# Attention with a feed-forward layer on one core: the order of the row-tiled group, of the division, and which pairs run it

## The chip, the cores and the metric

The kernel runs on one core of one Trainium2 chip. The time is the device time of one execution in microseconds (us). A core has five engines that run beside each other: TensorE (PE in the profile; its weight loads are listed as PEld), VectorE (DVE), ScalarE (ACT), GpSimd (POOL) and SyncE (SP). Each works through its own queue in order and waits on semaphores for the others. DMA transfers are issued by SP and by POOL.

## The reference

Attention with a relative position bias, 8 batches of 8 heads, 576 tokens, head size 64, and behind it two dense layers with a leaky ReLU between them on the 4608 tokens (512 to 2048 to 512).

```python
scores = scale * np.matmul(q, k.transpose(0, 1, 3, 2))
...
scores = scores + bias.transpose(2, 0, 1)[None, :, :, :]
scores = scores - np.max(scores, axis=-1, keepdims=True)
attn = np.exp(scores)
attn = attn / (np.sum(attn, axis=-1, keepdims=True) + 1e-09)
attn_out = np.matmul(attn, v)
x = attn_out.transpose(0, 2, 1, 3).reshape(B * S, H * D)
h = x @ w_in
g = np.maximum(0.01 * h, h)
out = g @ w_out
```

## The kernel before

**Pairs.** The work is cut into 32 items, each a batch and a pair of heads; item n is batch n // 4, heads 2p and 2p + 1 with p = n % 4. "Pair n" is item n below, counted from 0, so the 9th pair is n = 8 and the 13th is n = 12. While the scores of pair n are computed, the values of pair n - 1 are.

**Attention of a pair.** `score(n, u)` has PE compute a block of transposed scores (keys in the partitions) and ScalarE its exponential into `at`. Blocks u = 0 to 3 are 128 keys of both heads against 512 queries (L312): two products of 64 rows each, one per head, one on each half of the rows of the array. They use the two buffers of `ps_s` in turn. Block 4 (L305) is the last 64 queries; it is written to the banks o0 and o1 (`ps_q`). Block 5 (L315, L316) is the last 64 keys of both heads, with all 128 rows. `band(n, u)` multiplies the bias factor into the middle of a block on DVE (L348). The values of a head have a column of ones, so the row sum comes out beside the result. `av_tails` (L361) are the products of the last 64 keys into o0 and o1, row-tiled (each on 64 of the 128 rows), and `av` (L372) the others with all rows, a head after the other. `divide` (L380, L381) takes reciprocals and multiplies, which fills `opair`. `x_transposes` turns `opair` into `xT`, the tokens' input of the dense layers: by DMA from SP (L421), or for some pairs on PE (L428) with a copy on DVE (L429). `transpose_q` and `transpose_k` (L290, L294) make the next pair's `qt` and `kt`, from pair 9 on out of `turned`, which a DMA from SP fills (`turn_by_dma`, L265) after DVE has packed the rows (`pair_rows`, L257).

**The dense layers.** They are cut into pieces of four products of 512 columns and put between the steps of the pairs. An "in" piece (`ffn_in`, L454) is 128 of the 2048 hidden units for a tile of 512 tokens and ends in a leaky ReLU on ScalarE (`leaky`, L467). An "out" piece (`ffn_out`, L481) is a quarter of the sum for 128 tokens; the fourth is followed by a copy to `y` on DVE (L499) and a store from SP (L500). They use the two banks of tag "m", and now and then o0 (`spare`). `plan(n)` decides how many pieces a pair gets (seven or eight from pair 7 on) and what kind may run; what is over when the pairs are done runs in `moe_rest`.

**Two bodies.** `body_in_halves` is run for a pair where `both(n)` holds: in the program before for the 17 pairs n = 9, 13, 14, 17, 18, 19 and 21 to 31. There everything from score block 0 to score block 4 is row-tiled. The value products are split into two halves of the rows (`av_phase`): in phase 0 rows 0 to 63 work for the first head, into o0, while rows 64 to 127 work for the second, into o1; in phase 1 the other way round. Beside them an "in" and an "out" piece are done in halves in the same way (`open_two`, L598 and L601): a phase has four steps c, each of two products of 512 columns on the two halves of the rows. The two halves may not write the same bank at once, so phase 1 has to wait for the end of phase 0: `fence` puts an instruction on SP that waits for the last product of phase 0 (L389), and `behind` makes the first product of phase 1 wait for that. There are two such fences in a pair, for the values and for the pieces. All other pairs go through the body in the loop at the end, where `av` runs with all 128 rows between row-tiled scores and tails; there the first head is divided before the second one's products. Pairs 8 and 12 run there with the plan `lead`: eight out pieces, of which four stand between the value products (`slot`), with the copy to `y` on ScalarE.

**Order.** The order on every engine is the order in which the program issues (`manual_schedule`). So what is written first waits first, and what stands behind it in the same engine's queue waits with it.

Of the kernel before, what the change touches and what calls it, by code (L numbers as in the profile page):

```python
# [37 lines left out]
def kernel(  # L38
# [221 lines left out]
    def by_dma(n):  # L260
        return n > 2 * n_pairs
# [103 lines left out]
    def av(n, e):  # L365
        b, p = items[n]
        at = at_[n % 2]
        ps = outs[n][e][:, 0 : (NJ + 1) * (D + 1)].rearrange("p (i d) -> p i d", d=D + 1)
        for ic in range(NJ + 1):
            for c in range(NJ):  # L370
                o = (e * NJ + c) * S + ic * P
                nc.tensor.matmul(ps[:, ic, :], lhsT=at[:, o : o + P], rhs=vn[b % NBUF][:, c, 2 * p + e, :],  # L372
                                 start=False, stop=(ic == NJ and c == NJ - 1))
        divide(n, e)

    def divide(n, e):
        opair = ops_[n]
        ps = outs[n][e][:, 0 : (NJ + 1) * (D + 1)].rearrange("p (i d) -> p i d", d=D + 1)
        rcp = rc_pool.tile([P, NJ + 1, 1], FP32, name="rcp")
        nc.vector.reciprocal(rcp, ps[:, :, D : D + 1])  # L380
        nc.vector.tensor_tensor(out=opair[:, :, e * D : (e + 1) * D], in0=ps[:, :, 0:D],  # L381
                                in1=rcp.to_broadcast([P, NJ + 1, D]), op=ALU.mult)

    halves = (slice(0, P // 2), slice(P // 2, P))
    ended = mybir.DependencyInfo(mybir.DependencyClass.Sync, mybir.DependencyReason.DATA)
# [27 lines left out]
    def x_by_dma(n):  # L413
        return n_pairs + 2 <= n < N - 1 and n != 2 * n_pairs - 1

    def x_transposes(n):
        b, p = items[n]
        opair = ops_[n]
        w = (NJ + 1) * P
        if x_by_dma(n):  # L420
            nc.sync.dma_start_transpose(  # L421
                out=xT[p][:, b * S : b * S + w].rearrange("p (i t) -> p i t", t=P),
                in_=opair.rearrange("p i d -> p (i d)"),
            )
            return
        ps = ps_m_pool.tile([P, 8 * P], BF16, name="ps_tx", tag="m")
        for ic in range(NJ + 1):
            nc.tensor.transpose(ps[:, ic * P : (ic + 1) * P], in_=opair[:, ic, :], identity=ident)  # L428
        nc.vector.tensor_copy(out=xT[p][:, b * S : (b + 1) * S], in_=ps[:, 0:S])  # L429
# [28 lines left out]
    def leaky(T, f, pm, by_vector=False, between=None):  # L458
        g = gts[T][:, f, :]
        if by_vector:  # L460
            low = low_pool.tile([P, TT], BF16, name="low")
            nc.vector.tensor_scalar(low, pm, 0.01, None, op0=ALU.mult)
            if between is not None:
                between()
            nc.vector.tensor_tensor(out=g, in0=low, in1=pm, op=ALU.max)
        else:
            nc.scalar.activation(g, pm, AF.Prelu, bias=0.0, scale=1.0, alpha=0.01)  # L467
# [50 lines left out]
    def step(kind):  # L518
        T, s = made[kind], at_piece[kind]
        at_piece[kind] = (s + 1) % n_fc  # L520
        if at_piece[kind] == 0:
            made[kind] += 1
        return T, s

    def piece_out():
        T, s = step("out")
        ffn_out(T, s)
# [52 lines left out]
        elif room["left"] > room["keep"]:  # L580
            moe(1)

    def open_two():

        (Ti, f), (To, s) = step("in"), step("out")
        assert s % 4 == 0 and f < n_fc
        if f == 0:
            gts[Ti] = gt_pool.tile([P, n_fc, TT], BF16, name="gt")
        pi, po = bank("pm1"), bank("pm2")
        outs_pm[To] = po  # L590
        ti, ts = Ti * TT, (s // 4) * P

        def phase(k, lo, hi, last=None):
            for c in range(lo, hi):
                for r in range(2):
                    h = halves[r]
                    if r == k:
                        m = nc.tensor.matmul(pi, lhsT=w_in_sb[h, c, f * P : (f + 1) * P], rhs=xT[c][h, ti : ti + TT],  # L598
                                         start=(k == 0 and c == 0), stop=(k == 1 and c == n_cc - 1))
                    else:  # L600
                        m = nc.tensor.matmul(po, lhsT=gts[To][h, c, ts : ts + P], rhs=w_out_sb[h, c, :],  # L601
                                         start=(k == 0 and c == 0), stop=False)
                    if last is not None:
                        behind(m, last)
                        last = None
            return m

        return phase, lambda: leaky(Ti, f, pi)

    def both(n):  # L610
        return (by_dma(n) and n < N and can("in") and can("out") and at_piece["out"] % 4 == 0
                and not room["only"] and not room["split"] and not room["lead"] and room["left"] >= 6)

    def body_in_halves(n):

        loads(n)
        turns = rows_ahead(n) if by_dma(n + 1) else []
        for u in range(2):
            score(n, u)
        av_tails(n - 1)  # L620
        last = fence(av_phase(n - 1, 0))
        phase, low = open_two()
        phase(0, 0, 2)
        av_phase(n - 1, 1, last)
        if n + 1 < N:
            transpose_q(n + 1)
        band(n, 0)
        divide(n - 1, 0)
        divide(n - 1, 1)
        last = fence(phase(0, 2, n_cc))  # L630
        score(n, 2)
        score(n, 3)
        phase(1, 0, n_cc, last)
        band(n, 1)
        if n + 1 < N:
            transpose_k(n + 1)
        score(n, 4)
        low()
        for m in turns:
            turn_by_dma(m)  # L640
        x_transposes(n - 1)
        while stores:
            o, y = stores.pop(0)
            nc.sync.dma_start(out=o, in_=y)
        if not x_by_dma(n - 1):
            finished(n - 1)
        band(n, 2)
        piece_out()
        band(n, 4)
        score(n, 5)  # L650
        band(n, 5)
        piece_out()
        piece_out()
        room["left"] -= 5
        moe(room["left"], 0)

# [99 lines left out]
    def score(n, u):  # L756
        exp(n, u, qk_mm(n, u))
# [69 lines left out]
    for n in range(n_pairs + 1, N + 1):  # L827
        live = n < N
        more = n + 1 < N
        if x_by_dma(n - 2):  # L830
            finished(n - 2)
        plan(n)
        if live and both(n):
            body_in_halves(n)
            continue
        if live:
            begin(n)
            ps_a, ps_b = qk_mm(n, 0), qk_mm(n, 1)
# [48 lines left out]
        block = moe_block()  # L887
        next(block)
        exp(n, 3, ps_b)
        next(block)  # L890
        exp(n, 4, ps_c)
        if can("out"):
            next(block)
        band(n, 4)
        ps_a = qk_mm(n, 5)
        exp(n, 5, ps_a)
        band(n, 5)
        for _ in block:
            pass
# [31 lines left out]
```

## Time and profile before

| | |
|---|---|
| Time, median of 3 runs | 375.07 us (373.76, 375.07, 375.43) |
| The profiled execution's own time | 374.44 us |
| Its span | 372.5 us |
| PE busy | 358.1 us (96%) |
| ACT busy | 241.4 us (65%) |
| DVE busy | 198.8 us (53%) |
| Mean granted TensorE clock | 1.000 |

The span runs from the first to the last instruction, and the times of the views count from its start. In a row of the timeline stand the start, the length, the engine, the line, the operation with what it writes and reads, the number of instructions merged, and in brackets how long the engine had been idle before it and what ended that. A product's end is modelled, and products overlap, so the cost of a product is read from the start of one to the start of the next. Some products have no record, so a count can be one or two short. In the view of waits a row has the engine and line that waited, what it waited for, the total in us, how often, and the longest.

### The profile page before, as it was taken

The page shows a single profiled execution, that of the slowest core. Times are in us where ns is not written, and L with a number is a line of the kernel's source. Part 1 is how long each engine was busy: PE and PEld are TensorE (multiplying, and loading weights), DVE is VectorE, ACT ScalarE, POOL GpSimd, SP SyncE. Part 2 cuts the span into 40 slices and gives each one's busy share as a digit, 9 for nine tenths or more (in the row PEclk, how much of TensorE's full clock was granted, in tenths as well). Part 3 has the DMA queues.
Part 4 walks back from the last instruction along what each step waited for, and adds up shares of the span by engine and source line. Part 5 has one row for each costly group of instructions (what it writes and reads, how often), then busy time and mean ns, then how long its engine had stood idle before and what let it go on. Part 6 is the DMA issues. An engine that isn't in the chain of part 4 may idle for free.

```text
span 372.5 us, 10359 instructions
## 1 busy us (share of the span) xinstructions
PE 358.1 (96%) x4375; PEld 187.1 (50%) x4420; DVE 198.8 (53%) x502; ACT 241.4 (65%) x376; POOL 74.4 (20%) x118
## 2 busy tenths in 40 slices
PE   7889999999999999999999999999999999999995
PEld 2455555555455555555555554555555544444442
DVE  4688477777758576766766666665554200200221
ACT  5998887568856787777877776777777365054000
POOL 8764422233023203320232023100000000000000
PEclk9999999999999999999999999999999999999999
DMA  8999999999499969999899379534111000200212
GB/s 106 188 167 170 207 206 151 204 149 147 80 119 132 150 107 128 128 117 168 97 121 145 84 112 143 111 75 62 43 48 48 30 28 2 78 34 2 85 56 85
DMA packets 104359, 40.16 MB, mean 108 GB/s; under 512 B 83185, under 2 KB 98809, under 8 KB 104313
## 3 DMA queue, kind: packets, MB, share of 16 engines
q0 software_dynamic: 53696, 18.36, 47.3%
q1 hardware_dynamic: 50472, 21.02, 28.0%
q8 instruction: 34, 0.56, 0.6%
q10 hardware_dynamic: 144, 0.13, 0.1%
q14 instruction: 13, 0.10, 0.1%
HBM read 37.68 MB, written 9.45 MB: 127 GB/s over the span
## 4 chain that ended last, share of the span: by engine, by line
PE 80%; DMA 12%; POOL 3%; issue 2%; DVE 1%; ACT 1%; DVEq 0%; POOLq 0%
PE pm L481 28%; PE pm L454 26%; PE ps_s L312 6%; PE ps_o L405 5%; PE pm L598 4%; PE pm L601 4%; DMA vn<-in_v_dram 3%; PE ps_o L372 3%; DMA qn<-in_q_dram 3%; DMA w_in_sb<-in_moe_w_in_dram 3%; DMA xT<-opair 2%; PE ps_s L315 1%; PE ps_o L361 1%; POOL vn L125 1%; PE ps_q L305 1%
## 5 line engine op out<-in xcount | busy, mean ns | idle before, releaser
L325 ACT ACTIVATE at<-ps_s 128x1024 bf16<-128x1024 f32 x128 | 124.2, 1028 | 18.1 <-PE ps_s L312 18.0
L467 ACT ACTIVATE gt<-pm 128x512 bf16<-128x512 f32 x138 | 82.8, 605 | 71.3 <-PE pm L454 70.8
L454 PE MATMUL pm<-xT,w_in_sb 128*128 128x512 bf16 x490 | 117.2, 379 | 1.3 <-DMA w_in_sb<-in_moe_w_in_dram 0.3
L481 PE MATMUL pm<-w_out_sb,gt 128*128 128x512 bf16 x482 | 113.2, 379 | 3.2 <-issue 2.7
L348 DVE TENSOR_TENSOR at<-at,hk 128x768 bf16<-128x768 bf16 (+3 forms) x160 | 70.6, 453 | 53.0 <-ACT at L325 34.6
L454 PEld LDWEIGHTS <-w_in_sb 128*128 128x128 bf16 x508 | 47.6, 98 | 55.1 <-issue 0.7
L481 PEld LDWEIGHTS <-gt 128*128 128x128 bf16 x508 | 46.4, 98 | 52.6
L499 DVE COPY y<-pm 128x512 f32<-128x512 f32 x33 | 22.8, 691 | 71.0 <-PE pm L481 68.2
L312 PE MATMUL ps_s<-qt,kt 64*128 64x512 bf16 x256 | 40.0, 380 | 3.6 <-ACT at L325 3.0
L598 PE MATMUL pm<-xT,w_in_sb 64*128 64x512 bf16 x136 | 37.7, 376 | 0.1
L601 PE MATMUL pm<-w_out_sb,gt 64*128 64x512 bf16 x136 | 37.7, 376 | 0.0
L381 DVE TENSOR_TENSOR opair<-ps_o,rcp 128x320 bf16<-128x320 f32 x64 | 31.5, 492 | 3.3
L119 POOL DMA_DIRECT2D vn<-in_v_dram x32 | 28.5, 897 | 10.0 <-PE ps_o L372 4.2
L729 POOL COPY tick<-opair 1x1 bf16<-1x1 bf16 x18 | 3.8, 210 | 131.5 <-DVE opair L381 69.8
L380 DVE RECIPROCAL rcp<-ps_o 128x5 f32<-128x5 f32 x64 | 12.2, 191 | 27.5 <-PE ps_o L372 21.4
L405 PE MATMUL ps_o<-vn,at 64*128 64x65 bf16 x1360 | 26.4, 190 | 0.0
L405 PEld LDWEIGHTS <-at 64*128 64x128 bf16 x1360 | 24.2, 94 | 3.9 <-SPq L389 2.6
L372 PE MATMUL ps_o<-vn,at 128*128 128x65 bf16 x600 | 23.2, 194 | 0.0
L372 PEld LDWEIGHTS <-at 128*128 128x128 bf16 x600 | 20.7, 97 | 4.1 <-issue 0.7
L312 PEld LDWEIGHTS <-kt 64*128 64x128 bf16 x256 | 9.8, 94 | 25.7 <-issue 17.3
L332 ACT ACTIVATE at<-ps_s 128x576 bf16<-128x576 f32 x32 | 21.8, 681 | 0.2 <-PE ps_s L316 0.2
L328 ACT ACTIVATE at<-ps_q 128x256 bf16<-128x256 f32 x64 | 21.3, 395 | 0.3 <-PE ps_q L305 0.2
(63 smaller groups left out, 240.5 us busy)
## 6 DMA issues: line engine op xcount, KB each, us to landing
out_dram<-y SPq DMA_DIRECT2D x35, 256.0 KB, 2.3
qn<-in_q_dram POOLq DMA_DIRECT2D x14, 288.0 KB, 6.3
kn<-in_k_dram POOLq DMA_DIRECT2D x14, 288.0 KB, 6.8
vn<-in_v_dram POOLq DMA_DIRECT2D x28, 128.0 KB, 6.3
w_in_sb<-in_moe_w_in_dram POOLq DMA_DIRECT2D x2, 1024.0 KB, 12.7
w_out_sb<-in_moe_w_out_dram POOLq DMA_DIRECT2D x2, 1024.0 KB, 15.8
qn<-in_q_dram POOLq DMA_DIRECT2D x4, 144.0 KB, 4.2
kn<-in_k_dram POOLq DMA_DIRECT2D x4, 144.0 KB, 4.5
```

Of the source, the lines that this page charges most:

```text
L119: nc.gpsimd.dma_start(out=vn[b % NBUF][:, c, h0:h1, 0:D], in_=v[b, h0:h1, c * P : (c + 1) * P, :].rearrange("h s d -> s h d"),)
L312: nc.tensor.matmul(ps[:, e, :], lhsT=kt[r, u * P : (u + 1) * P], rhs=qt[r, 0:512], start=True, stop=True)
L325: nc.scalar.activation(at[:, :, u, 0:512], ps, AF.Exp, scale=scale)
L348: nc.vector.tensor_tensor(out=o, in0=o, in1=m, op=ALU.mult)
L372: nc.tensor.matmul(ps[:, ic, :], lhsT=at[:, o : o + P], rhs=vn[b % NBUF][:, c, 2 * p + e, :], start=False, stop=(ic == NJ and c == NJ - 1))
L381: nc.vector.tensor_tensor(out=opair[:, :, e * D : (e + 1) * D], in0=ps[:, :, 0:D], in1=rcp.to_broadcast([P, NJ + 1, D]), op=ALU.mult)
L405: m = nc.tensor.matmul(outs[n][e][:, ic * (D + 1) : (ic + 1) * (D + 1)], lhsT=at[halves[r], o : o + P], rhs=vn[b % NBUF][halves[r], c, 2 * ...
L454: nc.tensor.matmul(pm, lhsT=w_in_sb[:, c, f * P : (f + 1) * P], rhs=xT[c][:, t0 : t0 + TT], start=(c == 0), stop=(c == n_cc - 1))
L467: nc.scalar.activation(g, pm, AF.Prelu, bias=0.0, scale=1.0, alpha=0.01)
L481: nc.tensor.matmul(pm, lhsT=gt[:, f, ts * P : (ts + 1) * P], rhs=w_out_sb[:, f, :], start=(f == 0), stop=(f == n_fc - 1))
L598: m = nc.tensor.matmul(pi, lhsT=w_in_sb[h, c, f * P : (f + 1) * P], rhs=xT[c][h, ti : ti + TT], start=(k == 0 and c == 0), stop=(k == 1 an ...
L601: m = nc.tensor.matmul(po, lhsT=gts[To][h, c, ts : ts + P], rhs=w_out_sb[h, c, :], start=(k == 0 and c == 0), stop=False)
```

## The change

In `body_in_halves` score block 1 moves behind the tails and the first value phase; between the first and second value phase stand then score block 1 and one step of the pieces instead of two steps, and the other three steps follow the second value phase. `divide` takes both heads at once: first both reciprocals, then both multiplications. `both` becomes `two_kinds`, which also lets in pairs 8 and 12: there two groups of out pieces are opened side by side instead of an in and an out piece. In pair 8 the tokens of pair 7, which are transposed on PE, are transposed later, between the out pieces and into bank o0.

```diff
-        divide(n, e)
-
-    def divide(n, e):
+        divide(n, (e,))
+
+    def divide(n, heads):
         opair = ops_[n]
...
+        of = [outs[n][e][:, 0 : (NJ + 1) * (D + 1)].rearrange("p (i d) -> p i d", d=D + 1) for e in heads]
+        rcps = [rc_pool.tile([P, NJ + 1, 1], FP32, name="rcp") for _ in heads]
+        for ps, rcp in zip(of, rcps):
+            nc.vector.reciprocal(rcp, ps[:, :, D : D + 1])
+        for e, ps, rcp in zip(heads, of, rcps):
+            nc.vector.tensor_tensor(out=opair[:, :, e * D : (e + 1) * D], in0=ps[:, :, 0:D],
+                                    in1=rcp.to_broadcast([P, NJ + 1, D]), op=ALU.mult)
...
-    def x_transposes(n):
+    def x_transposes(n, spare=None):
...
-        ps = ps_m_pool.tile([P, 8 * P], BF16, name="ps_tx", tag="m")
+        if spare is None:
+            ps = ps_m_pool.tile([P, 8 * P], BF16, name="ps_tx", tag="m")
+        else:
+            ps = ps_o_pool.tile([P, 8 * P], BF16, name="ps_tx", tag=spare)
...
+    def open_piece(kind, at=None):
+
+        if kind == "in":
+            T, f = step("in")
+            if f == 0:
+                gts[T] = gt_pool.tile([P, n_fc, TT], BF16, name="gt")
+            pm = bank("pm1")
+            return pm, [(w_in_sb[:, c, f * P : (f + 1) * P], xT[c][:, T * TT : (T + 1) * TT])
+                        for c in range(n_cc)], lambda: leaky(T, f, pm)
+        T, s = at or step("out")
+        ts, part = s // 4, s % 4
+        pm = outs_pm[T] = bank("pm2")
+        return pm, [(gts[T][:, f, ts * P : (ts + 1) * P], w_out_sb[:, f, :])
+                    for f in range(part * n_cc, (part + 1) * n_cc)], None
+
+    def side_by_side(one, two):
+
         def phase(k, lo, hi, last=None):
             for c in range(lo, hi):
                 for r in range(2):
...
+                    pm, steps, low = one if r == k else two
+                    w, x = steps[c]
+                    m = nc.tensor.matmul(pm, lhsT=w[halves[r]], rhs=x[halves[r]], start=(k == 0 and c == 0),
+                                         stop=(low is not None and k == 1 and c == n_cc - 1))
...
+    def two_kinds(n):
+
+        if n <= 2 * n_pairs - 1 or n >= N or room["only"] or at_piece["out"] % 4 or not can("out"):
+            return None
+        if room["lead"] and room["left"] == 8 and at_piece["out"] + 8 <= n_fc:
+            return "out", "out"
+        if can("in") and not room["split"] and not room["lead"] and room["left"] >= 6:
+            return "in", "out"
+        return None
+
+    def body_in_halves(n, kinds):
 
         loads(n)
         turns = rows_ahead(n) if by_dma(n + 1) else []
-        for u in range(2):
-            score(n, u)
+        score(n, 0)
         av_tails(n - 1)
         last = fence(av_phase(n - 1, 0))
-        phase, low = open_two()
-        phase(0, 0, 2)
+        score(n, 1)
+        T, s = made["out"], at_piece["out"]
+        if kinds[0] == "out":
+            one, two = open_piece("out", (T, s)), open_piece("out", (T, s + 4))
+        else:
+            one, two = open_piece("in"), open_piece("out")
+        phase = side_by_side(one, two)
+        phase(0, 0, 1)
         av_phase(n - 1, 1, last)
         if n + 1 < N:
             transpose_q(n + 1)
         band(n, 0)
-        divide(n - 1, 0)
-        divide(n - 1, 1)
-        last = fence(phase(0, 2, n_cc))
+        divide(n - 1, range(2))
+        last = fence(phase(0, 1, n_cc))
         score(n, 2)
         score(n, 3)
         phase(1, 0, n_cc, last)
...
         score(n, 4)
-        low()
+        if kinds[0] == "in":
+            one[2]()
         for m in turns:
             turn_by_dma(m)
-        x_transposes(n - 1)
+        if x_by_dma(n - 1):
+            x_transposes(n - 1)
...
         if not x_by_dma(n - 1):
-            finished(n - 1)
+            late = [n - 1]
+        else:
+            late = []
         band(n, 2)
+        if kinds[0] == "out":
+            outs_pm[T] = one[0]
+            ffn_out(T, s + 1)
+            band(n, 4)
+            score(n, 5)
+            band(n, 5)
+            ffn_out(T, s + 2)
+            ffn_out(T, s + 3)
+            for m in late:
+                x_transposes(m, "o0")
+                finished(m)
+            outs_pm[T] = two[0]
+            for part in range(5, 8):
+                ffn_out(T, s + part)
+            at_piece["out"] = (s + 8) % n_fc
+            made["out"] += at_piece["out"] == 0
+            return
...
-        if live and both(n):
-            body_in_halves(n)
+        kinds = two_kinds(n)
+        if kinds:
+            body_in_halves(n, kinds)
             continue
```

More of the change, by code (lines that the diff above doesn't have):

```diff
@@ L373, in av @@
                                  start=False, stop=(ic == NJ and c == NJ - 1))
-        divide(n, e)
-    def divide(n, e):
+        divide(n, (e,))
+    def divide(n, heads):
         opair = ops_[n]
[L378 to L382, printed above, removed]
+        of = [outs[n][e][:, 0 : (NJ + 1) * (D + 1)].rearrange("p (i d) -> p i d", d=D + 1) for e in heads]
[5 more added lines that the diff above has]
+                                    in1=rcp.to_broadcast([P, NJ + 1, D]), op=ALU.mult)
     halves = (slice(0, P // 2), slice(P // 2, P))
@@ L581, in slot @@
             moe(1)
[L583 to L591, printed above, removed]
+    def open_piece(kind, at=None):
[12 more added lines that the diff above has]
+    def side_by_side(one, two):
         def phase(k, lo, hi, last=None):
@@ L595, in phase @@
                 for r in range(2):
[L596 to L602, printed above, removed]
+                    pm, steps, low = one if r == k else two
+                    w, x = steps[c]
+                    m = nc.tensor.matmul(pm, lhsT=w[halves[r]], rhs=x[halves[r]], start=(k == 0 and c == 0),
+                                         stop=(low is not None and k == 1 and c == n_cc - 1))
                     if last is not None:
@@ L606, in phase @@
             return m
[L608 to L614, printed above, removed]
+        return phase
+    def two_kinds(n):
[7 more added lines that the diff above has]
+    def body_in_halves(n, kinds):
         loads(n)
         turns = rows_ahead(n) if by_dma(n + 1) else []
-        for u in range(2):
-            score(n, u)
+        score(n, 0)
         av_tails(n - 1)
         last = fence(av_phase(n - 1, 0))
-        phase, low = open_two()
-        phase(0, 0, 2)
+        score(n, 1)
[6 more added lines that the diff above has]
+        phase(0, 0, 1)
         av_phase(n - 1, 1, last)
@@ L653, in body_in_halves @@
         piece_out()
+        for m in late:
+            x_transposes(m, "o1")
+            finished(m)
         room["left"] -= 5
```

## The prediction

> **What bounds the kernel now.** I read the page first: the busy shares, the granted clock, the chain that ended last.
>
> ```profile
> PE 358.1 (96%) x4375; PEld 187.1 (50%) x4420; DVE 198.8 (53%) x502; ACT 241.4 (65%) x376; POOL 74.4 (20%) x118
> ...
> PEclk9999999999999999999999999999999999999999
> ...
> PE 80%; DMA 12%; POOL 3%; issue 2%; DVE 1%; ACT 1%; DVEq 0%; POOLq 0%
> ```
>
> TensorE (PE) is busy nearly always, its clock is granted in full, and it holds most of the chain. A busy PE can still hide gaps, so next I took the timeline of one steady pair (n = 28) on PE alone. The first column is the start in us.
>
> ```profile
> 251.86 0.61 PE L312 MATMUL ps_s<-qt,kt 64*128 64x512 bf16 x4
> 252.30 0.32 PE L361 MATMUL ps_o<-v,at 64*128 64x65 bf16 x10
> 252.46 0.78 PE L405 MATMUL ps_o<-vn,at 64*128 64x65 bf16 x40
> 253.06 0.37 PE L598 MATMUL pm<-xT,w_in_sb 64*128 64x512 bf16 x1
> ...
> 253.49 0.78 PE L405 MATMUL ps_o<-vn,at 64*128 64x65 bf16 x40
> 254.11 0.37 PE L598 MATMUL pm<-xT,w_in_sb 64*128 64x512 bf16 x1
> ...
> 254.54 0.60 PE L312 MATMUL ps_s<-qt,kt 64*128 64x512 bf16 x4
> 254.97 0.38 PE L601 MATMUL pm<-w_out_sb,gt 64*128 64x512 bf16 x1
> ...
> 255.83 0.28 PE L305 MATMUL ps_q<-qt,kt 64*128 64x64 bf16 x8
> ...
> 258.89 2.75 PE L454 MATMUL pm<-xT,w_in_sb 128*128 128x512 bf16 x12
> 261.58 0.39 PE L312 MATMUL ps_s<-qt,kt 64*128 64x512 bf16 x2
> ```
>
> Read by starts. Four steps of the second phase, two products of 512 columns side by side in each, take 255.83 - 254.97 = 0.86 us, so a step costs 0.215. Score blocks 2 and 3 take 0.43, two steps' worth. The tails take 0.16, each value phase 0.60 to 0.62. From 251.86 to 255.83, 3.97 us, nothing is left over: twelve steps (2.58) plus 0.16, 0.60 and 0.62 make 3.96. The change of tiling shows at the edge: twelve full products (2.58) occupy 258.89 to 261.58, 2.69, so about 0.1 us is lost on entering the row-tiled group, once per pair. The whole pair lasts 261.58 - 251.86 = 9.72. So the row-tiled group of the 17 pairs that run it is already packed, and a new order inside it has almost nothing to win.
>
> Next, the waits that the two fences make:
>
> ```profile
> PEld L601 <- SPq L389: 2.7, 17, 0.2
> ...
> PEld L405 <- SPq L389: 2.6, 17, 0.2
> ```
>
> and one of them in the timeline of pair 28, with the division that follows on VectorE (DVE):
>
> ```profile
> 253.32 0.82 PEld L405 LDWEIGHTS <-at 64*128 64x128 bf16 x40 [0.15 <-SPq L389]
> ...
> 254.31 0.20 DVE L380 RECIPROCAL rcp<-ps_o 128x5 f32<-128x5 f32 x1 [0.38 <-PE ps_o L405]
> ...
> 254.60 0.49 DVE L381 TENSOR_TENSOR opair<-ps_o,rcp 128x320 bf16<-128x320 f32 x1
> ...
> 255.01 0.18 DVE L380 RECIPROCAL rcp<-ps_o 128x5 f32<-128x5 f32 x1
> ...
> 255.22 0.49 DVE L381 TENSOR_TENSOR opair<-ps_o,rcp 128x320 bf16<-128x320 f32 x1
> ```
>
> It is the weight load that waits for the fence, until 253.32, while the products before it stream until 253.49: the wait is covered, with 0.17 us to spare. Tighter is the division: score block 4 (L305) writes the two banks that the division reads, the division ends at 255.22 + 0.49 = 255.71, and block 4 starts at 255.83. That is 0.12 us of slack.
>
> **The change, part by part.**
>
> The new order in the 17 pairs. Before, score 0, score 1, tails, phase 0, two steps, phase 1, two steps; after, score 0, tails, phase 0, score 1, one step, phase 1, three steps. No instruction is added or lost. What lies between a value phase and its fence's waiter is two steps' worth in both (score block 1 counts as one, 0.215), so the 0.17 us of spare stays. Block 1 comes 0.76 us later (0.16 + 0.60); its exponential stands behind that of block 0:
>
> ```profile
> 252.46 1.93 ACT L325 ACTIVATE at<-ps_s 128x1024 bf16<-128x1024 f32 x2
> ```
>
> ScalarE needs 0.97 for each and turns to block 1 at 253.43. Block 1 starts at 252.08 + 0.76 = 252.84 and is 0.39 long (the last row of the pair above), so it is ready by 253.23, and the bank that score 3 needs is free when it was. The value phases end one step (0.215) earlier, so the division has 0.12 + 0.215 of slack and more. There is one boundary more between kinds of products; such a boundary cost 0.44 - 0.43 = 0.01 at score to tails. I bound this part at -0.02 to +0.02 a pair, -0.35 to +0.35 over 17, and take 0, the nearest row.
>
> Both reciprocals first. The first product starts 0.29 after the reciprocal that it needs, and the second reciprocal now falls in that gap; the second product follows 0.41 after the first (as 67.68 follows 67.28 below), so the chain is 0.29 + 0.41 + 0.49 = 1.19 us instead of 1.40. Nobody waits for it in the 17 pairs, so it is worth nothing there.
>
> Pair n = 12 joins the row-tiled group. Its timeline on PE, and ScalarE at its start:
>
> ```profile
> 101.64 0.60 PE L312 MATMUL ps_s<-qt,kt 64*128 64x512 bf16 x4
> 102.49 0.33 PE L361 MATMUL ps_o<-v,at 64*128 64x65 bf16 x10 [0.24 <-ACT gt L467]
> ...
> 111.99 0.39 PE L312 MATMUL ps_s<-qt,kt 64*128 64x512 bf16 x2
> ```
>
> ```profile
> 101.31 1.13 ACT L467 ACTIVATE gt<-pm 128x512 bf16<-128x512 f32 x2
> ```
>
> It lasts 10.35 and holds the same eight FFN pieces as pair 28 (9.72). Of the 0.63 between them, 0.41 is this: the tails start 0.85 after score 0 where pair 28 shows 0.44, since they write bank o0, which the activation of the previous pair's last piece still reads until 101.31 + 1.13 = 102.44. The other 0.22 is two more changes of tiling. After the change the tails come directly behind score 0, and are held until 102.49 all the same. So the pair will be 0.85 + (9.72 - 0.22) = 10.35: the 0.22 saved on tiling is given back at o0, since block 1 no longer covers that wait. Worth 0.
>
> Pair n = 8 joins too. On PE:
>
> ```profile
> 65.20 0.60 PE L312 MATMUL ps_s<-qt,kt 64*128 64x512 bf16 x4
> ...
> 71.33 0.45 PE L428 MATMUL ps_tx<-ident,opair 128*128 128x128 bf16 x5
> 71.62 1.89 PE L481 MATMUL pm<-w_out_sb,gt 128*128 128x512 bf16 x7
> ...
> 75.41 0.39 PE L312 MATMUL ps_s<-qt,kt 64*128 64x512 bf16 x2
> ```
>
> It lasts 10.21 with five transposes (71.62 - 71.33 = 0.29), which stay, only later and into o0. By PE alone it would be 9.72 + 0.29 = 10.01, a gain of 0.20. But its DVE queue changes order, and here is a wait:
>
> ```profile
> 65.31 0.69 DVE L499 COPY y<-pm 128x512 f32<-128x512 f32 x1 [0.72 <-PE pm L481]
> ...
> 66.72 0.35 DVE L257 COPY pr<-kn 96x768 bf16<-96x768 bf16 x1
> ...
> 67.28 0.49 DVE L381 TENSOR_TENSOR opair<-ps_o,rcp 128x320 bf16<-128x320 f32 x1
> 67.68 0.41 DVE L348 TENSOR_TENSOR at<-at,hk 128x512 bf16<-128x512 bf16 x1
> 68.26 0.67 DVE L290 COPY qt<-tu 128x576 bf16<-128x576 bf16 x1 [0.16 <-DMA tu<-pr]
> ```
>
> ```profile
> 59.81 2.11 SPq L265 DMA_TRANSPOSE tu<-pr  x1
> ```
>
> The copy of q for pair 9 (L290) waited for the DMA that turns it, issued at 59.81 and landed at about 68.24. In the old order only 0.16 us of DVE time was lost, since the first division and the band stood ahead. In the new body `transpose_q` stands ahead of the band and of both divisions. The four `pr` copies end at 66.72 + 0.35 = 67.07; DVE then stands until 68.24, and queued behind the waiting copy are the band, both reciprocals and both products. An instruction starts about 0.08 before the one ahead has ended (67.28 + 0.49 against 67.68), so: copy 0.59, band 0.33, division 1.19, together 2.11 from 68.26, to 70.37. Score block 4, which writes the banks under division, is due at 65.20 + 3.97 = 69.17. PE stands there for 1.20 us, with all of its later work behind it, and nothing after it gives that back, since PE is the bound. Had the old division chain of 1.40 held, it would be 1.41. If the turn landed by 67.07 there would be no stall: between, it counts one for one. Pair 8: 10.01 + 1.20 = 11.21, that is 1.00 more than now.
>
> A rule bears on that landing. The turns of pairs 10 and 11 are queued next:
>
> ```profile
> 66.56 4.14 SPq L265 DMA_TRANSPOSE tu<-pr  x2
> ```
>
> They move behind the second fence, to about 68.2, so they no longer compete with the turn of pair 9. The Trainium skill ("DMA: Bandwidth & Descriptors", section "Issuing engines are not separate DMA queues") says that DMAs of all issuing engines run on the same 16 engines and interleave. By that the landing comes earlier, and the stall shrinks towards the first rival below; the trace cannot show by how much. Work on the queues otherwise: the turn of pair 10 is read in pair 9 at about 65.20 + 11.21 + 1.3 = 77.7; issued at 68.2 and as slow as that of pair 9 (8.4), it lands at 76.6, so it is covered by 1 us. The y copies of the two out groups, both on DVE now at 0.69 each, lie beside seven pieces of PE work; that of pair 7's last piece ends at 66.00, and the first step needs its bank at 65.20 + 0.22 + 0.16 + 0.60 + 0.22 = 66.40.
>
> The sum: 0 for the 17 pairs, 0 for pair 12, +1.00 for pair 8. The profiled execution took 374.44 us at a span of 372.5; it becomes 375.4. The median of the three runs shown is 375.07, so I forecast 376.1.
>
> **The rivals.** First: the turn of pair 9 lands in time. How turns land:
>
> ```profile
> DMA to landing us min/median/max: 3.3/4.1/7.4
> ```
>
> That of pair 9 took 8.4, over all the others with a record, and it must take under 7.3 for the stall to vanish. For this speak the other landings and the two turns taken out of its way; against it, that this DMA was issued before anything that the change touches. Then the sum is -0.20: 374.9.
>
> Second, ending clearly slower: the first fence loses its cover. Its weight load is released 253.32 - 252.46 = 0.86 after the value phase starts. If score block 1, which now stands in that gap, hides under the end of the phase and covers nothing, phase 1 is ready at 0.60 + 0.215 = 0.82 and waits 0.04 by these rows, or, as an estimate that doubles this for the load itself, 0.08, in each of 19 pairs: 0.8 to 1.5 us on top of the forecast, 376.9 to 377.6. It decides once block and step together last under 0.26. Against it: blocks 0 and 1 take a full 0.44 before, with tails right behind.
>
> Third: the new order wins 0.1 us in every one of 19 pairs, 1.9 in all, so 373.2 or less. Against it, the 3.97 us without a gap.
>
> **How the numbers follow.** Forecast (stall of 0.5 to 1.9 us) 0.56; turn in time or nearly 0.24; fence 0.13; gain in every pair 0.07. About 0.5%, 1.9 us, is what a measurement of this kernel can tell from no change, as the runs shown spread by 1.7. Faster by more: the third rival and a little of the first, 0.08. Slower by more: the second, 0.13, and the part of the forecast where the turn lands 0.9 later still, 0.14, together 0.27. Within: 0.65. The range starts below the first rival with its unknown 0.35 and some spread, at 374.2, and goes to the upper part of the second, 377.6.
>
> **What would show it.** In the trace after, L290 of pair 9 near 68 us with over 1 us idle before it, ended by the DMA; then L305 on PE some 1.2 us late, released by DVE L381. Pair 12 still held at its tails, by about 0.6 between score 0 and tails. Pairs like n = 28 at 9.72 within 0.02. I am wrong if pair 8 lasts under 10.3 (the turn landed early), if a steady pair moves by 0.05 (fence or order), or if PE stands anywhere else.

## The result, and the profile after

The changed kernel takes 375.84 us in the median of 20 runs, the kernel before 374.90 in 20 runs beside it; the ratio is 1.0034, with a 95% interval of 1.0018 to 1.0051. So it is slower by a third of a per cent, 0.7 to 1.9 us. The forecast was 376.1. Every ratio here and below counts all executions but one of g3, a slow one of 941 us. The profiled execution took 375.74 us (374.44 before), at a span of 374.0 (372.5 before). The page, in the lines that answer to those quoted of before:

```profile
PE 362.5 (97%) x4516; PEld 187.5 (50%) x4516; DVE 196.5 (53%) x504; ACT 240.8 (64%) x374; POOL 77.3 (21%) x118
...
PEclk9999999999999999999999999999999999999998
...
PE 89%; ACT 4%; DVE 4%; DMA 2%; issue 1%; DVEq 0%; ACTq 0%
```

PE is still the bound at full clock, so the time must be sought in gaps of PE. The steady pair n = 28, PE alone (start, length, engine, line):

```profile
252.49 0.39 PE L312 MATMUL ps_s<-qt,kt 64*128 64x512 bf16 x2
252.72 0.32 PE L361 MATMUL ps_o<-v,at 64*128 64x65 bf16 x10
252.87 0.78 PE L407 MATMUL ps_o<-vn,at 64*128 64x65 bf16 x40
253.47 0.39 PE L312 MATMUL ps_s<-qt,kt 64*128 64x512 bf16 x2
...
253.91 0.78 PE L407 MATMUL ps_o<-vn,at 64*128 64x65 bf16 x40
...
256.46 0.28 PE L305 MATMUL ps_q<-qt,kt 64*128 64x64 bf16 x8
...
262.21 0.39 PE L312 MATMUL ps_s<-qt,kt 64*128 64x512 bf16 x2
```

It lasts 262.21 - 252.49 = 9.72, as before, and score block 4 comes 3.97 after score 0, as before. The fences' waits, by line:

```profile
PEld L610 <- SPq L391: 3.0, 19, 0.2
PEld L407 <- SPq L391: 3.0, 19, 0.2
```

Nineteen pairs now, each still 0.16 at the weight loads, under running products. Pair 8, first PE, then DVE:

```profile
65.31 0.39 PE L312 MATMUL ps_s<-qt,kt 64*128 64x512 bf16 x2
...
69.29 0.28 PE L305 MATMUL ps_q<-qt,kt 64*128 64x64 bf16 x8
...
75.31 0.39 PE L312 MATMUL ps_s<-qt,kt 64*128 64x512 bf16 x2
```

```profile
66.83 0.35 DVE L257 COPY pr<-kn 96x768 bf16<-96x768 bf16 x1
67.10 0.64 DVE L290 COPY qt<-tu 128x576 bf16<-128x576 bf16 x1
67.67 0.41 DVE L348 TENSOR_TENSOR at<-at,hk 128x512 bf16<-128x512 bf16 x1
68.00 0.25 DVE L381 RECIPROCAL rcp<-ps_o 128x5 f32<-128x5 f32 x2
68.28 0.89 DVE L383 TENSOR_TENSOR opair<-ps_o,rcp 128x320 bf16<-128x320 f32 x2
```

In this execution the copy of q did not wait: the turn of pair 9 had landed by 67.10. Block 4 came on time, and the pair lasted 10.00. The gap in PE is elsewhere, in pair 25, at the step that needs the tokens of pair 23:

```profile
224.57 0.37 PE L610 MATMUL pm<-xT,w_in_sb 64*128 64x512 bf16 x1
...
225.81 0.37 PE L610 MATMUL pm<-xT,w_in_sb 64*128 64x512 bf16 x1 [0.86 <-DMA xT<-opair]
```

The two starts lie 1.24 apart instead of 0.215, so PE lost 1.03 there. Before, the same place lost 0.30:

```profile
224.67 0.38 PE L598 MATMUL pm<-xT,w_in_sb 64*128 64x512 bf16 x1
...
225.18 0.37 PE L598 MATMUL pm<-xT,w_in_sb 64*128 64x512 bf16 x1
```

Then there is the end of the program, from the last product to the end of the span: 4.59 us after, 3.80 before. Of the 1.4 us between the two spans (373.96 and 372.54), +0.72 is pair 25, +0.79 the end, -0.21 pair 8, and +0.11 lies ahead of pair 8. So the sum came out as forecast, but not by the forecast's term: two of the prediction's own signs of being wrong are here, pair 8 under 10.3 and PE standing elsewhere. That called for experiments.

### The profile page after: what moved, and what is told of

Read it like the earlier page. It is cut to its first block, busy times and chain, and to the rows that moved or that the text cites. A ratio compares the mean times of both kernels' runs of the same rounds, so it can differ in the third digit from the quotient of the medians.

```text
span 374.0 us, 10606 instructions
## 1 busy us (share of the span) xinstructions
PE 362.5 (97%) x4516; PEld 187.5 (50%) x4516; DVE 196.5 (53%) x504; ACT 240.8 (64%) x374; POOL 77.3 (21%) x118
## 4 chain that ended last, share of the span: by engine, by line
PE 89%; ACT 4%; DVE 4%; DMA 2%; issue 1%; DVEq 0%; ACTq 0%
PE pm L486 28%; PE pm L459 28%; PE pm L610 8%; PE ps_s L312 7%; PE ps_o L407 6%; PE ps_o L372 4%; DMA xT<-opair 2%; ACT at L325 2%; PE ps_s L315 2%; PE ps_o L361 1%; PE ps_w L750 1%; DVE opair L383 1%; PE ps_t L275 1%; PE ps_tx L433 1%; PE ps_q L305 1%; DVE at L348 1%
## 5 line engine op out<-in xcount | busy, mean ns | idle before, releaser
L486 PEld LDWEIGHTS <-gt 128*128 128x128 bf16 x492 | 45.0, 98 | 51.4
L312 PE MATMUL ps_s<-qt,kt 64*128 64x512 bf16 x256 | 43.2, 380 | 3.4 <-ACT at L325 3.0
L610 PE MATMUL pm<-w_out_sb,gt 64*128 64x512 bf16 x168 | 42.2, 376 | 0.0
L383 DVE TENSOR_TENSOR opair<-ps_o,rcp 128x320 bf16<-128x320 f32 x64 | 29.7, 488 | 1.6
L407 PE MATMUL ps_o<-vn,at 64*128 64x65 bf16 x1520 | 29.5, 190 | 0.0
L407 PEld LDWEIGHTS <-at 64*128 64x128 bf16 x1520 | 27.1, 94 | 4.4 <-SPq L391 3.0
L312 PEld LDWEIGHTS <-kt 64*128 64x128 bf16 x256 | 11.6, 94 | 25.3 <-issue 16.5
L381 DVE RECIPROCAL rcp<-ps_o 128x5 f32<-128x5 f32 x64 | 10.0, 182 | 22.3 <-PE ps_o L372 19.3
L372 PE MATMUL ps_o<-vn,at 128*128 128x65 bf16 x520 | 20.1, 194 | 0.0
L372 PEld LDWEIGHTS <-at 128*128 128x128 bf16 x520 | 17.9, 97 | 3.5 <-issue 0.7
```

Of the source, the lines that this page charges most:

```text
L312: nc.tensor.matmul(ps[:, e, :], lhsT=kt[r, u * P : (u + 1) * P], rhs=qt[r, 0:512], start=True, stop=True)
L407: m = nc.tensor.matmul(outs[n][e][:, ic * (D + 1) : (ic + 1) * (D + 1)], lhsT=at[halves[r], o : o + P], rhs=vn[b % NBUF][halves[r], c, 2 * ...
L486: nc.tensor.matmul(pm, lhsT=gt[:, f, ts * P : (ts + 1) * P], rhs=w_out_sb[:, f, :], start=(f == 0), stop=(f == n_fc - 1))
L610: m = nc.tensor.matmul(pm, lhsT=w[halves[r]], rhs=x[halves[r]], start=(k == 0 and c == 0), stop=(low is not None and k == 1 and c == n_cc ...
```

## The experiments

Three theories. The copy theory is the prediction's: in pair 8 the wait for the turn of pair 9 stands ahead of the division and holds score block 4. The landing theory: tokens land too late for pairs 13 or 25 because loads are queued beside them. The order theory: every pair pays a little. The fetch theory came later, for the end. All ratios are to the kernel before, measured beside it on the same chip; e1 to e4, f1 to f4 and g1 to g4 each shared a chip. The stretches are from each kernel's one profile: starts of score 0 from pair to pair, and the end as above. What lies ahead of pair 8 also differs between executions (its start lies between 64.9 and 67.5 us over the 14 profiles), so the spans of single profiles differ by that as well.

| kernel | pair 8 | pair 12 | pair 13 | pair 25 | end | ratio (95%) |
|---|---|---|---|---|---|---|
| before | 10.21 | 10.34 | 8.86 | 10.03 | 3.80 | 1 |
| changed | 10.00 | 10.35 | 8.86 | 10.75 | 4.59 | 1.0034 (1.0018 to 1.0051) |
| e1 changed again | 11.33 | 10.35 | 9.02 | 11.09 | 4.47 | 1.0051 (1.0033 to 1.0069) |
| e2 order only | 10.21 | 10.34 | 8.89 | 9.99 | 3.78 | 1.0005 (0.9990 to 1.0019) |
| e3 pairs only | 10.17 | 10.13 | 9.64 | 10.56 | 4.47 | 1.0045 (1.0027 to 1.0063) |
| e4 loads by second head | 10.00 | 10.35 | 8.86 | 9.93 | 4.53 | 1.0029 (1.0011 to 1.0048) |
| f1 division first | 10.00 | 10.35 | 9.70 | 9.81 | 4.70 | 1.0015 (0.9996 to 1.0034) |
| f2 pair 8 only | 10.00 | 10.34 | 8.86 | 10.45 | 3.78 | 1.0003 (0.9985 to 1.0021) |
| f3 pair 12 only | 10.21 | 10.35 | 8.88 | 10.76 | 3.97 | 1.0016 (0.9998 to 1.0034) |
| f4 turn sooner | 11.33 | 10.35 | 9.43 | 10.14 | 4.48 | 1.0042 (1.0023 to 1.0062) |
| g1 ScalarE padded | 10.00 | 10.35 | 9.49 | 10.35 | 4.47 | 1.0035 (1.0012 to 1.0057) |
| g2 before, three fewer | 10.21 | 10.34 | 9.05 | 10.22 | 3.97 | 1.0006 (0.9984 to 1.0027) |
| g3 all waits away | 10.00 | 10.35 | 8.86 | 9.72 | 3.78 | 0.9975 (0.9950 to 1.0000) |
| g4 loads behind tokens | 10.00 | 10.35 | 8.86 | 9.72 | 3.77 | 0.9979 (0.9959 to 0.9999) |

**e1, the changed kernel once more.** No edit.

> The changed kernel once more, as the yardstick of this call. All theories: ratio to before 1.002 to 1.005. Landing theory (the tokens of pair 23 land too late for the third-last step of pair 25, since the loads queued beside them now start 0.3 us sooner): pair 25 stands 0.6 to 1.3 us on PE, against 0.3 before, pair 8 takes 10.0. Copy theory (the prediction's: in pair 8 the copy of q waits for the turn of pair 9 and delays the division): pair 8 takes 10.3 to 11.2, pair 25 about 10.0.

The same program, another execution, and here the forecast stall stands in full. DVE and PE of pair 8:

```profile
66.74 0.35 DVE L257 COPY pr<-kn 96x768 bf16<-96x768 bf16 x1
68.40 0.65 DVE L290 COPY qt<-tu 128x576 bf16<-128x576 bf16 x1 [1.31 <-DMA tu<-pr]
...
69.59 0.89 DVE L383 TENSOR_TENSOR opair<-ps_o,rcp 128x320 bf16<-128x320 f32 x2
```

```profile
70.14 0.20 PE L305 MATMUL ps_q<-qt,kt 64*128 64x64 bf16 x1 [0.78 <-DVE opair L383]
70.53 0.27 PE L305 MATMUL ps_q<-qt,kt 64*128 64x64 bf16 x7 [0.20 <-DVE opair L383]
```

DVE stands 1.31 us on the DMA; from the copy's start to the division's end it is 69.59 + 0.89 - 68.40 = 2.08 (2.11 forecast); the products of block 4 that need both banks start at 70.53, 1.34 after their due time of 65.22 + 3.97. The pair lasts 11.33, where 11.21 was forecast. Pair 25 lost 1.37 in the same execution. Both theories are live: the wait in pair 8 is there in one execution of the same program and not in the other, and that in pair 25 differs in size.

**e2, the order alone.** Pairs 8 and 12 go back to the old body.

```diff
-        if n <= 2 * n_pairs - 1 or n >= N or room["only"] or at_piece["out"] % 4 or not can("out"):
+        if n <= 2 * n_pairs or n >= N or room["only"] or at_piece["out"] % 4 or not can("out"):
             return None
-        if room["lead"] and room["left"] == 8 and at_piece["out"] + 8 <= n_fc:
-            return "out", "out"
```

> The new order and both reciprocals first, but only in the 17 pairs that ran the group before; pairs 8 and 12 run the old body. Landing theory: ratio 1.002 to 1.006, no better than the changed kernel, since pair 25 still stands 0.6 us or more; it lacks the 0.2 us won in pair 8. Copy theory: the loss is gone, ratio 0.999 to 1.001. A cost of the order in every pair would show as pairs longer than 9.72 and a ratio as that of the changed kernel.

1.0005, no change, and the steady pair keeps its 9.72. The order theory falls: the new order and the early reciprocals cost and win nothing in the 17 pairs. The landing theory in its first form falls with it, since the loads start as early here as in the changed kernel (3.35 us after the start of pair 24) and pair 25 loses only 0.27, about what it lost before. In e3 below it is the other way round: the loads start as late as in the kernel before (3.57), and pair 25 loses 0.84.

**e3, the pairs alone.** Pairs 8 and 12 in the group, the old order and division everywhere.

```diff
-        score(n, 0)
-        av_tails(n - 1)
-        last = fence(av_phase(n - 1, 0))
-        score(n, 1)
+        score(n, 0)
+        score(n, 1)
+        av_tails(n - 1)
+        last = fence(av_phase(n - 1, 0))
...
-        phase(0, 0, 1)
+        phase(0, 0, 2)
...
-        divide(n - 1, range(2))
-        last = fence(phase(0, 1, n_cc))
+        divide(n - 1, (0,))
+        divide(n - 1, (1,))
+        last = fence(phase(0, 2, n_cc))
```

> Pairs 8 and 12 in the row-tiled group, but the old order and the old division everywhere. Landing theory: the first product of a division comes as late as before, so do the loads, and pair 25 stands 0.3 us; pair 8 wins 0.2; ratio 0.999 to 1.001. Copy theory: the full loss stays or grows (division chain of 1.40): ratio 1.003 to 1.006.

1.0045: the loss is all here, against the landing theory's 0.999 to 1.001. It comes from admitting pairs 8 and 12. The profile shows two more things. The turn was in time, and yet pair 8 lasts 10.17, not 10.00: with the old chain the division alone is late for block 4, so the early reciprocals (with the earlier value phases) are worth 0.17 in that pair. And pair 12 lasts 10.13, not 10.35:

```profile
102.80 0.60 PE L312 MATMUL ps_s<-qt,kt 64*128 64x512 bf16 x4
103.64 0.33 PE L361 MATMUL ps_o<-v,at 64*128 64x65 bf16 x10 [0.24 <-ACT gt L472]
```

Score blocks 0 and 1 stand together in the 0.84 us in which the tails wait for o0. In the changed kernel the wait is as long, with one block in it:

```profile
101.55 0.39 PE L312 MATMUL ps_s<-qt,kt 64*128 64x512 bf16 x2
102.39 0.33 PE L361 MATMUL ps_o<-v,at 64*128 64x65 bf16 x10 [0.45 <-ACT gt L472]
```

**e4, later loads.**

```diff
-        nc.gpsimd.tensor_copy(out=tick, in_=ops_[n - 2][0:1, 0, 0:1])
+        nc.gpsimd.tensor_copy(out=tick, in_=ops_[n - 2][0:1, 0, D : D + 1])
```

> The changed kernel, but the small GpSimd copy that holds back the loads of the next batch reads a number of the second head of the finished pair, not of the first, so the loads start 0.4 us later, about where they started before. Landing theory: pair 25 stands 0.3 us again and the ratio falls to 0.998 to 1.001. Copy theory: no change against the changed kernel, 1.002 to 1.005.

The loads of pair 24 start 0.7 us later than in the changed kernel, 0.5 later than before (4.06 after the pair's start). Pair 25 loses 0.21 in the profile, but the ratio stays at 1.0029: so small a delay of the loads does not restore the time.

**f1, the division ahead of the copy of q in pair 8.**

```diff
-        if n + 1 < N:
+        if n + 1 < N and n != 2 * n_pairs:
             transpose_q(n + 1)
         band(n, 0)
         divide(n - 1, range(2))
+        if n == 2 * n_pairs:
+            transpose_q(n + 1)
```

> The changed kernel, with one move: in pair 8 the copy of q for pair 9 stands behind the division, not ahead of it. Copy theory (the wait for the turn of pair 9 stands ahead of the division and holds score block 4): pair 8 takes 10.0 in the profile, and the ratio to before falls from about 1.004 to 0.998 to 1.001. If the loss is not there (tokens landing late at pairs 13 and 25): 1.002 to 1.005 as the changed kernel.

Between the two: 1.0015, with an interval that holds both no loss and the changed kernel's 1.0034, so the ratio does not tell whether the copy's wait is part of the loss. The trace tells more. By the record of its semaphore the turn landed at 67.55, while DVE would have come to the copy at 66.70 in the changed kernel's order; by the forecast's chain that would have cost pair 8 about 0.8 us (an estimate). With the division first it kept its 10.00. Pair 13 lost 0.84 in this profile, and the end was 4.70.

**f2, pair 8 alone, and f3, pair 12 alone.**

```diff
 # f2
-        if room["lead"] and room["left"] == 8 and at_piece["out"] + 8 <= n_fc:
+        if n == 2 * n_pairs and room["lead"] and room["left"] == 8 and at_piece["out"] + 8 <= n_fc:
 # f3
-        if n <= 2 * n_pairs - 1 or n >= N or room["only"] or at_piece["out"] % 4 or not can("out"):
+        if n <= 2 * n_pairs or n >= N or room["only"] or at_piece["out"] % 4 or not can("out"):
```

> The changed kernel, but pair 12 runs the old body. Copy theory: all of the loss stays, 1.002 to 1.005, with pair 8 anywhere from 10.0 to 11.4 in one profile. Token theory (pair 12 in the group turns pair 11's tokens into a heap of loads, so pair 13 waits): the loss is gone, 0.999 to 1.001.

> The changed kernel, but pair 8 runs the old body. Copy theory: the loss is gone, 0.999 to 1.001, pair 8 takes 10.2. Token theory: 1.002 to 1.005, with pair 13 longer than 8.9.

Neither shows the loss of both: 1.0003 and 1.0016, though the second one's interval just reaches 1.0034. Pair 8 alone thus costs little on the average, which the copy theory did not expect. The token theory was right on f2, but missed on f3, where the ratio fell short of 1.002 and pair 13 took 8.88. The end column gives a hint: it is long only where both pairs are in (g3 and g4 below have both and a short end).

**f4, the turn of pair 9 issued sooner.**

```diff
             begin(n)
+            if n == 2 * n_pairs - 1:
+                turn_ahead(n)
...
             band(n, 0)
-            turn_ahead(n)
+            if n != 2 * n_pairs - 1:
+                turn_ahead(n)
```

> The changed kernel, but the turn of pair 9's rows is issued at the start of pair 7, some 3 us sooner, so that it has landed when pair 8 reads it; the order in pair 8 stays. Copy theory: pair 8 takes 10.0, no idle time before its copy of q, ratio 0.998 to 1.001 like the kernel with the division first. If the place in the DVE queue cost something without the wait: 1.002 to 1.005.

It was meant to take the wait away and did not:

```profile
57.44 1.72 SPq L265 DMA_TRANSPOSE tu<-pr  x1
```

```profile
68.17 0.65 DVE L290 COPY qt<-tu 128x576 bf16<-128x576 bf16 x1 [1.31 <-DMA tu<-pr]
```

Issued 2.4 us sooner than in the kernel before (59.81), the turn landed at about 68.15, where it landed there too (68.24). It took 10.7 us. The landing did not follow the issue. What it goes with can be read from the other traces: the last load of k that GpSimd issues at about the same time, here in the kernel before and in the changed one, each with its time to landing:

```profile
59.90 0.67 POOL L112 DMA_DIRECT2D kn<-in_k_dram  x1 [0.94 <-DMA kn<-in_k_dram]
```

```profile
DMA to landing us min/median/max: 7.3/7.3/7.3
```

```profile
57.20 0.67 POOL L112 DMA_DIRECT2D kn<-in_k_dram  x1 [0.71 <-DMA kn<-in_k_dram]
```

```profile
DMA to landing us min/median/max: 7.4/7.4/7.4
```

The load landed at 67.25 and 64.64, and the turn at 68.24 and 65.90 by the records of its semaphore, though it was issued at 59.81 and 59.92. In all 13 profiles with the usual issue the turn landed 1.0 to 1.3 us behind that load. In f4 it was issued ahead of the load and landed with it (68.14 and 68.19). No run moved this load alone, so it is a reading of traces, not a test.

**g1, three more instructions on ScalarE, and g2, three fewer in the kernel before.** The change takes ScalarE's y copies from pairs 8 and 12. In the stretch from the last product to the end, the DMA queues were read before and after (packets, MB, share of the window; the last store is issued from ScalarE's queue, ACTq):

```profile
q1 hardware_dynamic: 144, 0.13, 10.3%
q10 hardware_dynamic: 144, 0.13, 10.1%
...
out_dram<-y ACTq DMA_DIRECT2D x1, 128.0 KB, 1.8
```

```profile
q10 hardware_dynamic: 144, 0.13, 8.9%
q1 hardware_dynamic: 144, 0.13, 8.7%
q14 instruction: 2, 0.02, 1.0%
...
out_dram<-y ACTq DMA_DIRECT2D x1, 128.0 KB, 2.6
```

After the change two packets of instructions (8 KB each) arrive in this stretch, and the last store lands 2.6 us after its issue, not 1.8. So the fetch of instructions was suspected, ScalarE's first.

```diff
 # g1
-    nc.scalar.activation(warm, warm, AF.Exp)
+    for _ in range(4):
+        nc.scalar.activation(warm, warm, AF.Exp)
 # g2, on the kernel before
-        copy = nc.scalar.copy if j % 3 == 2 else nc.vector.tensor_copy
+        copy = nc.vector.tensor_copy
```

> The changed kernel with three more tiny ScalarE instructions at its start, which restores the number that ScalarE had before (the change takes one y copy of each of pairs 8 and 12 from it). Fetch theory (with three fewer, a fetch of ScalarE's instructions falls beside the last store): the stretch from the last product to the end falls from 4.5 to 4.7 to 3.8 us, and the ratio to before by about 0.002, to 1.000 to 1.003. If another engine's instructions or the stores themselves lengthen the end, it stays at 4.5 to 4.7.

> The kernel before, with the three small copies that ScalarE makes for the bias table at the start given to VectorE: three fewer instructions on ScalarE, three more on VectorE, nothing else. Fetch theory: the end grows from 3.8 to 4.5 us or more, and the ratio is 1.001 to 1.003. Otherwise the end stays at 3.8 and the ratio at 0.999 to 1.001.

ScalarE it is not. g1 removed one of the two fetches and the end stayed at 4.47; g2 brought one in, 2.25 us after the last product, and the end was 3.97. What holds in all 14 profiles is this: where a fetch starts 1.9 to 2.1 us after the last product, the last packet of the last store ends about 1.0 us behind that start, at 2.88 to 3.10, and the end takes 4.47 to 4.70 (seven kernels). Where none does, that packet ends at 2.30 to 2.32 and the end takes 3.77 to 3.97 (seven). A fetch at 2.25, when the store is all but over, does no such thing (g2, g4). Whose the early fetch is stays open, and no run moved it alone. The traces give a pointer. Counted with waits and semaphores, VectorE has 578 instructions in those seven and 574 to 577 in the others, and no other engine's count parts them; in the same way the fetch at 2.24 to 2.37 is there in just the eight profiles in which ScalarE has 579.

**g3, all known waits away, and g4, only the loads held.**

```diff
 # g3 and g4
-        nc.gpsimd.tensor_copy(out=tick, in_=ops_[n - 2][0:1, 0, 0:1])
+        nc.gpsimd.tensor_copy(out=tick, in_=xT[items[n - 2][1]][0:1, items[n - 2][0] * S : items[n - 2][0] * S + 1])
 # g3 has the edits of f1 and g1 too
```

> The changed kernel with the division ahead of the copy of q in pair 8, the three ScalarE instructions, and the loads held until the tokens of the finished pair have landed (the small GpSimd copy reads xT, not opair). If the three waits make up the loss: pair 8 10.0, pair 13 8.86, pair 25 9.72, end 3.8, and a ratio of 0.996 to 0.999, below both kernels. If loads so late make other waits: pairs elsewhere grow and the ratio is 1.000 or more.

> The changed kernel, with only the loads held until the tokens of the finished pair have landed. Landing theory: pairs 13 and 25 fall to 8.86 and 9.72 and the ratio by 0.001 to 0.003 against the changed kernel, to 1.000 to 1.003; pair 8 and the end stay as they are (10.0 to 11.3, 4.5 to 4.7). If landing does not depend on the loads, pair 25 stays between 9.8 and 11.1.

Both lie below the two kernels, 0.9975 and 0.9979, if only just clear of the kernel before by their intervals (g3's ends at 1.0000). For g4 that is more than was forecast, as the end, too, was short. GpSimd's queue in pair 24, changed kernel and g4:

```profile
215.72 0.18 POOL L772 COPY tick<-opair 1x1 bf16<-1x1 bf16 x1 [15.98 <-DVE opair L383]
215.95 0.68 POOL L112 DMA_DIRECT2D qn<-in_q_dram  x1
```

```profile
220.02 0.18 POOL L772 COPY tick<-xT 1x1 bf16<-1x1 bf16 x1 [15.22 <-DMA xT<-opair]
220.56 1.33 POOL L112 DMA_DIRECT2D qn<-in_q_dram  x1 [0.36 <-DVE y L504]
```

The loads start 4.6 us later and no longer lie beside the tokens' transfer. How that transfer lands, over its 24 issues (min/median/max), changed kernel and g4:

```profile
DMA to landing us min/median/max: 2.5/4.7/8.6
```

```profile
DMA to landing us min/median/max: 2.6/3.9/6.5
```

And the one that pair 25 waits for, in the kernel before, the changed kernel and g4:

```profile
DMA to landing us min/median/max: 8.1/8.1/8.1
```

```profile
DMA to landing us min/median/max: 8.6/8.6/8.6
```

```profile
DMA to landing us min/median/max: 2.8/2.8/2.8
```

It lands 2.8 after its issue instead of 8.6, and pairs 13 and 25 lose nothing, not even the 0.31 that pair 25 lost before the change. Here the landing theory holds in its broader form: not 0.3 us of shift, but the loads beside the transfer are what makes it late. g4 leaves the order of pair 8 alone and has no early fetch at the end (3.77; its edit also leaves VectorE with 574 instructions), so its distance from g1 on the same chip (0.9979 against 1.0035) is not landing alone.

## Why the prediction was right, and where not

**The 17 pairs: 0.** Right, by the trace (9.72 and 3.97 again) and by e2 (1.0005). The cover of the first fence holds, so the second rival falls; so does the third, the gain in every pair.

**Pair 12: 0.** Right in size and mechanism: 10.34 before and 10.35 after, the tails held 0.84 behind score 0. e3 shows both sides, since with block 1 ahead of the tails the pair wins the 0.21. What the step left out is its neighbour. In pair 12's new body the transfer of pair 11's tokens is issued when it was, 5.0 us after the pair's start, but other transfers move closer to it: GpSimd's loads start 3.98 after the pair's start instead of 3.01, and a turn on SP's queue 3.62 instead of 0.67. GpSimd's first load, before and after:

```profile
104.66 0.82 POOL L112 DMA_DIRECT2D qn<-in_q_dram  x1
```

```profile
105.52 0.67 POOL L112 DMA_DIRECT2D qn<-in_q_dram  x1
```

Pair 13 lasted 8.86 to 9.70 in the eight profiles with pair 12 in the group and the loads not held behind the tokens (mean 9.24), against 8.86 to 9.05 in the four with pair 12 in the old body. With the loads held (g3, g4) it took 8.86.

**Pair 8: +1.00.** The chain is as forecast where the wait occurs: 1.31 of idle DVE, 2.08 of chain, 11.33 for the pair. But it occurs in two of the seven profiles that have that order with the new division; in the others the pair wins its 0.21. The step that failed is the one that took the landing at 68.24 of a single execution as the landing. It was given 0.56 as a case; in the sum it should have been a term with a chance. The records of the turn's semaphore give it: in the 13 profiles with the usual issue the turn landed 5.0 to 8.6 us after its issue, and in five of them (before, e1, f1, f3, g2) later than 1.8 us after pair 8's start, when DVE comes to the copy in the new order. At one for one the mean stall over the 13 is 0.4 us, so with the 0.21 won the term was worth about +0.2 (an estimate), not +1.00. None of the reasons weighed named what the landing goes with, GpSimd's load of k. Taking the turns of pairs 10 and 11 out of the way did nothing that can be seen: where they are issued before this one lands (before, f3, g2), it lands 1.0 to 1.2 us behind that load, and 1.0 to 1.3 elsewhere. The Trainium skill's rule in "DMA: Bandwidth & Descriptors" ("Issuing engines are not separate DMA queues"), that all DMAs share 16 engines and interleave, agrees with f4, where an earlier issue gave no earlier landing (68.15 against 68.24), and with g4, where the loads of another queue set when the tokens land (2.8 us after their issue instead of 8.6).

**What made up the sum instead.** Two terms were missing: later tokens in pairs 13 and 25, and 0.7 us at the end. An estimate from the table sets the means of the seven kernels that have both pairs in and the loads not held (changed, e1, e3, e4, f1, f4, g1) against those of the three with neither pair in (before, e2, g2): +0.19 in pair 8, -0.02 in pair 12, +0.35 in pair 13, +0.30 in pair 25 and +0.68 at the end, 1.5 us in all, where the runs of the changed kernel show 0.7 to 1.9. The loss belongs to pairs 8 and 12 together (e3 1.0045, e2 1.0005, f2 1.0003, f3 1.0016), and the end is long only with both, so the end is a fitting part of it. That the early fetch makes it long is argued from the traces and not shown by a run, and its share in executions without a profile was not measured, nor how often pair 8 stalls in them. That the forecast of 376.1 met 375.84 is thus partly luck: a term that is there now and then was counted in full, and two that were not seen filled the rest.

## What to carry to other kernels

When a group of instructions joins another body, list for each in-order queue which DMA-fed instruction now stands ahead of the one that frees the bound engine's buffer; here a copy that had 0.16 us of harmless wait came ahead of a division with none to spare. Take a landing time out of one profile as a draw, not as a constant: before it goes into a sum, look at the same transfer in several executions (5.0 to 8.6 us for the turn of pair 9) or at its like over the program (2.5 to 8.6 for the tokens), and at what lands just ahead of it. Here, holding back the large loads beside one late small transfer won (g4, 0.9979), and issuing another sooner did not bring its landing forward (f4, 1.0042).

## What was not expected of the hardware

The turn of pair 9 landed 1.0 to 1.3 us behind a load of GpSimd's in 13 profiles, whether the load landed at 64.6 or at 67.3. Issued 2.4 us sooner it landed no sooner than in the kernel before, 68.15 against 68.24. A transfer of instructions, 8 KB, that starts 1.9 to 2.1 us after the last product, beside the last store, goes with an end 0.5 to 0.9 us longer, in seven profiles of seven; one that starts at 2.25 does not. If the early one is the cause, a few instructions more or less in one engine's stream can move the program's end by 0.2%.
